# Moving SBUF addresses: the first x pair beside the weight chunks, kvs 32 bytes on, and weight chunks at a pitch of 4128 bytes instead of 4096

## The chip, the cores and the metric

The kernel runs on one core of a Trainium2 chip. The metric is the device time of one execution in microseconds; for the kernel before the median of three runs is 907.83 us (906.24 to 909.28). One more execution was taken with the hardware profiler, and the trace and the profile's page are of that one.

## The reference

An attention without a score matrix is followed by a two-layer feed-forward network. With batch 8, 8 heads, 576 positions and head size 64, and all in float32:

```
q_s = softmax(q, over d);  k_s = softmax(k, over positions)
kv  = einsum('bhsd,bhse->bhde', k_s, v)        # 64 x 64 for each head
x   = einsum('bhsd,bhde->bhse', q_s, kv)       # to [4608, 512]
out = max(x @ w_in, 0)**2 @ w_out              # 512 -> 2048 -> 512
```

## The kernel before

**Precision.** TensorE's fast four-byte type, float32r, keeps fewer bits than float32. So each operand of the network is split into a high part and a low remainder, and every product is made of three matmuls: high by high, low by high, high by low. A product costs three matmuls of 128x128 weights by 512 columns.

**Blocks.** The 4608 positions are handled in nine blocks of 512: block b (0 to 7) is the first 512 positions of batch b, and block 8 gathers the 64 positions left over of each batch. A block has 16 steps, one for each slice `fc` of 128 of the 2048 hidden features. A step has two halves of 12 matmuls. In the first, `ffn_h` with `h_part` (lines 406 to 408), the weights in the array are 128x128 slices of the chunk `wi[fc]`, and the moving operand is the block's x: `x_hi` in lines 406 and 408, `x_lo` in line 407, four slices `cc` each. In the second, `ffn_out` (lines 440 to 442), the weights in the array are slices of the activations `g_hi` and `g_lo`, and the moving operand is the chunk `wo[fc]`. So a chunk `wi` is what is loaded into the array, and a chunk `wo` is what streams through it. The two halves of a step belong to slices two apart (`LAG`).

**Two x pairs.** `x_hi` and `x_lo` exist twice. Blocks 0, 2, 4, 6 and 8 read the first pair, `x_hi0` and `x_lo0`, blocks 1, 3, 5 and 7 the second one, `x_hi1` and `x_lo1`. The attention of batch b runs in the steps of block b-1 and writes the other pair. Its matmuls are those of lines 299 (k by v, plain float32) and 378 (q by kv, with `kvs` as the weights and `qs` as the moving operand, 320 or 256 columns), put between the steps' matmuls by the table `slots`. Block 7's steps hold the gathering of the leftovers and no attention; block 8 holds neither.

**Weights.** Each of the 32 chunks (16 `wi`, 16 `wo`) is loaded once as raw float64 words, turned into a float32 and split into a high half (2048 bytes per partition) and a low half (2048 bytes) in the same place; this happens during the attention of batch 0 and in block 0. In order of loading the chunks are i0, i1, i2, i3, o2, i4, o3, i5, o0, i6, o1, i7, o4, i8, o5, i9, o6, i10, o7, i11, o8, i12, o9, i13, o10, i14, o11, i15, o12, o13, o14, o15; call that place n, from 0 to 31.

**Where the tiles lie.** A tile takes the same bytes in every partition. Pools lie one behind another in the order in which they are opened, and the tiles in a pool in the order of their first use, each rounded up to 32 bytes. From the sizes one can count, per partition:

- the 32 chunks lie end to end at a pitch of 4096 bytes;
- `x_hi0`, the first tile of the pool `const`, lies 79,008 bytes below the first chunk, which is 32 bytes off a multiple of 64; `x_lo0` follows after 8192 bytes;
- `x_hi1` and `x_lo1` lie right behind the last chunk, 131,072 and 139,264 bytes above the first chunk, both multiples of 4096;
- the tiles `g_hi`, `g_lo` and `qs` lie at multiples of 64 bytes from the first chunk; `kvs` lies 46,112 bytes below it, again 32 off a multiple of 64.

`qe`, the transposed q of pairs 1 and 3 of batch 0, is a tile of the pool `first` (2304 bytes), the topmost; `w_pool` has a tag `raw` of four buffers of 2560 bytes through which passing tiles go (`left`, `xf`, `tb`, `xs`, `o`).

Of the kernel before, what the change touches and what calls it, by code (L numbers as in the profile page):

```python
# [8 lines left out]
F32 = mybir.dt.float32  # L9
F32R = mybir.dt.float32r  # L10
U32 = mybir.dt.uint32
# [5 lines left out]
P = 128  # L17
# [7 lines left out]
RAWB, WB = 4, 3  # L25
EARLY_SPLITS = [("o",2),("o",3),("i",4),("o",0)]
OFFSET = 100
AHEAD = 4
EARLY = 8
PRE = 4  # L30
# [12 lines left out]
def attention_ffn_kernel(ctx: ExitStack, tc: tile.TileContext, q, k, v, w_in, w_out, out):  # L43
    nc = tc.nc

    B, H, S, D = q.shape
    DM, DF = w_in.shape
    NPAIR = H // 2
    NCC = DM // P
    NFC = DF // P  # L50
    NT = 512
# [3 lines left out]
    const = ctx.enter_context(tc.tile_pool(name="const", bufs=1))  # L55
    work = ctx.enter_context(tc.tile_pool(name="work", bufs=2))
    attn_pool = ctx.enter_context(tc.tile_pool(name="attn", bufs=2))
    w_pool = ctx.enter_context(tc.tile_pool(name="weights", bufs=2))
    dram = ctx.enter_context(tc.tile_pool(name="dram", bufs=1, space=bass.MemoryType.DRAM))
    ps_a = ctx.enter_context(tc.tile_pool(name="ps_a", bufs=1, space=bass.MemoryType.PSUM))  # L60


    stay = ctx.enter_context(tc.tile_pool(name="stay", bufs=1))
    raws, wi, wo = {}, {}, {}
    x_hi = [const.tile([P, NCC, NT], F32R, name="x_hi0")]
    x_lo = [const.tile([P, NCC, NT], F32R, name="x_lo0")]
    x_left = dram.tile([P, NCC, B * LEFT], F32, name="x_left")


# [10 lines left out]
    def next_bank(who):  # L80
        n = taken[who]
        taken[who] += 1
        return banks[{"first": n % 3, "h": n % 2, "a": 2 + n % 2}[who]]

    kvs = const.tile([P, 2, P], F32R, name="kvs")
    qT = const.tile([P, 4, LOW, BLK], F32, name="qT")
    ident = const.tile([P, P], F32, name="ident")
    start = ExitStack()
    first = start.enter_context(tc.tile_pool(name="first", bufs=1))
    ps_first = start.enter_context(tc.tile_pool(name="ps_first", bufs=2, space=bass.MemoryType.PSUM))  # L90
    for i in range(NB, NPAIR):
        kt.append(first.tile([P, 2, LOW, D], F32, name=f"kt{i}"))
        vt.append(first.tile([P, 2, LOW, D], F32, name=f"vt{i}"))
        qt.append(first.tile([P, 2, LOW, D], F32, name=f"qt{i}"))
    ones = const.tile([P, 1], F32, name="ones")

    v0 = [t.rearrange("p h j d -> p (h j d)")[:, : 2 * LOW * D].rearrange("p (h j d) -> p h j d", h=2, j=LOW) for t in vt]

# [38 lines left out]
    def load_pair(b, pr):  # L137
        for n in range(3):
            load_one(b, pr, n)

    chunks, last = [], []

    def load_w(part, fc):
        raw = stay.tile([P, 512, 2], U32, name=f"raw_{part}{fc}", tag=f"{part}{fc}")
        if part == "i":
            src = w_in[:, fc * P : (fc + 1) * P].bitcast(U32).rearrange("(cc p) f -> p cc f", p=P)
            nc.sync.dma_start(raw.rearrange("p (cc f) w -> p cc (f w)", cc=NCC), src)
        else:
            nc.sync.dma_start(raw.rearrange("p f w -> p (f w)"), w_out[fc * P : (fc + 1) * P, :].bitcast(U32))
        raws[part, fc] = raw  # L150

    def split_weight(part, fc):

        raw = raws[part, fc]
        low, high = raw[:, :, 0], raw[:, :, 1]
        w = w_pool.tile([P, 512], U32, name="w", bufs=WB)
        wf = w.bitcast(F32)

        with ExitStack() as order:
            if his:
                order.enter_context(tc.issue_after(his[-1].ins))
            nc.scalar.activation(low, raw.bitcast(U8)[:, :, 3], AF.Copy, scale=1 / 32, bias=-15.5 / 32)
        t = banks[3]
        nc.scalar.activation(t, high.bitcast(F32), AF.Copy, scale=2.0**-112)
        t = t.bitcast(U32)
        nc.vector.scalar_tensor_tensor(out=t, in0=t, scalar=3, in1=low, op0=ALU.logical_shift_left, op1=ALU.bitwise_or)
        nc.vector.scalar_tensor_tensor(out=w, in0=high, scalar=0x80000000, in1=t, op0=ALU.bitwise_and, op1=ALU.bitwise_or)  # L169
        finish_split()  # L170
        chunk = stay.tile([P, 2, 512], F32R, name=f"w{part}{fc}", tag=f"{part}{fc}")
        chunks.append(chunk)
        (wi if part == "i" else wo)[fc] = chunk

        def parts():
            his.append(nc.scalar.copy(chunk[:, 0], wf))
            nc.gpsimd.tensor_tensor(chunk[:, 1], wf, chunk[:, 0].bitcast(F32), op=ALU.subtract)  # L177

        unsplit.append(parts)
# [3 lines left out]
    def finish_split():  # L183
        while unsplit:
            unsplit.pop()()
# [5 lines left out]
    def ordered(f, *args):  # L191

        with ExitStack() as order:
            if last:
                order.enter_context(tc.issue_after(last[-1].ins))
            return f(*args)

    def attention(b, pr):

        n = b * NPAIR + pr  # L200
# [5 lines left out]
        st = {}  # L206
        odd = early and n % 2 == 1

        def bank(cols):
            if b == 0 and odd:  # L210
                t = ps_first.tile([P, NT], F32, name="first_ps", tag="a")
            else:
                t = next_bank("first" if b == 1 else "a") if b else banks[2]
            return t[:, :cols]
# [120 lines left out]
        def q_t_early(j0, j1):  # L335
            def go():
                qn = st["qn"]
                if "q" not in st:
                    if b == 0 and odd:
                        st["q"] = first.tile([P, S], F32, name="qe")  # L340
                    else:
                        st["q"] = qT.rearrange("p g j a -> p (g j a)")[:, :S]
                c0, c1 = j0 * P, min(j1 * P, S)
                ps = bank(c1 - c0)
                for j in range(j0, j1):
                    if j < HIGH:
                        mm = nc.tensor.transpose(ps[:, j * P : (j + 1) * P], qn[:, j], ident)
                    else:
                        mm = nc.tensor.transpose(ps, qn[:HALF, HIGH], ident[:HALF, :HALF])
                if b:  # L350
                    last.append(mm)
                nc.scalar.copy(st["q"][:, c0:c1], ps)
            return go
# [128 lines left out]
    for c in LOADS:  # L482
        i = int(c[1])
        if c[0] == "w":
            load_w("i", i)
        else:
            load_one(0, i, "kqv".index(c[0]))
    order0 = list(range(2, PRE)) + list(range(min(2, PRE))) + list(range(PRE, NFC))

    def load_more(n):  # L490
        load_w("o", order0[n])
        if n + PRE < NFC:
            load_w("i", order0[n + PRE])

    for n in range(AHEAD):
        load_more(n)
    for t in range(len(us[0]) + SKEW * (NPAIR - 1)):
        for pr in range(NPAIR):
            n = t - SKEW * pr
            if 0 <= n < len(us[pr]):  # L500
                with tc.high_priority(OFFSET):
                    us[pr][n]()
                if n == 4:
                    split_weight("i", pr)
                    if pr == NPAIR - 1:
                        for c in EARLY_SPLITS:
                            split_weight(*c)
                if n == 7:
                    finish_split()
                    for fc in range(min(PRE, pr + 1)):  # L510
                        for cc in [pr] if fc < pr else range(pr + 1):
                            h_part(hs[fc], 0, fc, cc)
# [6 lines left out]
    for pr in range(NB):  # L519
        load_pair(1, pr)  # L520
    for n in range(AHEAD, NFC):
        load_more(n)
# [24 lines left out]
    def in_slot(i):  # L547
        for u in slots.get(i, []):
            if i < 2 * NFC:
                with tc.high_priority(OFFSET):  # L550
                    ordered(u)
# [3 lines left out]
    for n in range(len(steps) + LAG):  # L555
        if n < len(steps):
            blk, fc = steps[n]
            if n < PRE:
                gs[n] = activate(hs[fc], blk, fc)
            else:  # L560
                gs[n] = ordered(ffn_h, blk, fc) if blk == 0 else ffn_h(blk, fc)
            if blk == 0:
                for x in [n + 4] if n else range(5):
                    if PRE <= x < NFC and order0[x] not in wi:
                        split_weight("i", order0[x])
                for x in [n + 2] if n else range(3):
                    if x < NFC and order0[x] not in wo:
                        split_weight("o", order0[x])
                finish_split()
        m = n - LAG  # L570
        in_slot(2 * n)
        if m >= 0:
            b2, f2 = steps[m]
            if m % NFC == 0:
                accs[b2] = [ps_o.tile([P, DM], F32, name=f"o_ps{t}", tag="o") for t in range(4)]
            args = b2, f2, gs.pop(m), accs[b2], m % NFC
            ordered(ffn_out, *args) if b2 == 0 else ffn_out(*args)
        in_slot(2 * n + 1)
# [30 lines left out]
```

## Time and profile before

| | |
|---|---|
| median of the runs | 907.83 us |
| profiled execution, first to last instruction | 903.5 us |
| PE busy | 876.7 us (97%) |
| DVE, ACT, POOL busy | 579.4, 408.2, 201.9 us |
| mean granted TensorE clock | 0.991 |

The profiled span is 4.3 us below the median of the runs, which also holds what lies around the instructions. PE is TensorE's matmul, PEld its weight load, DVE VectorE, ACT ScalarE, POOL GpSimd. A matmul's record reaches until its results have drained, so records of neighbours overlap; what counts for the time is the distance from one start to the next.

### The profile page before, as it was taken

What the parts mean: (1) busy time and instruction counts of PE and PEld (TensorE: products, weight loads), DVE (VectorE), ACT (ScalarE), POOL (GpSimd) and SP (SyncE); (2) the same over time, 40 slices, a digit from 0 to 9 for tenths busy, and PEclk for the clock granted to TensorE, in tenths of its full rate; (3) what the DMA queues carried; (4) which work ended last, traced back from release to release, by engine and by line L of the source; (5) the groups of instructions that cost most, each with busy time, mean ns of one, the idle gap of its engine ahead of it and who ended that gap; (6) DMA issues with size and microseconds to landing.
All of it is one profiled execution on the core that took longest, in us unless ns stands there. A gap on an engine that the chain in (4) does not pass through costs nothing.

```text
span 903.5 us, 12672 instructions
## 1 busy us (share of the span) xinstructions
PE 876.7 (97%) x4368; PEld 703.5 (78%) x4368; DVE 579.4 (64%) x1177; ACT 408.2 (45%) x801; POOL 201.9 (22%) x177
## 2 busy tenths in 40 slices
PE   4898999999999999999999999999999999999997
PEld 3576677888878888888888888888888888888885
DVE  6767797877778776877688768876764242222222
ACT  3876765455444444544454444444444232222222
POOL 3666535222213220231122212221222000000000
PEclk9989999999999999999999999999999999999999
DMA  9898212422142223322333133222311030001001
GB/s 244 269 320 248 59 37 56 118 72 83 44 117 73 79 60 101 87 70 71 88 84 81 49 80 91 85 57 68 93 31 32 3 93 1 1 1 46 1 1 46
DMA packets 95743, 73.18 MB, mean 81 GB/s; under 512 B 47552, under 2 KB 85440, under 8 KB 95680
## 3 DMA queue, kind: packets, MB, share of 16 engines
q1 hardware_dynamic: 94944, 71.53, 28.9%
q10 hardware_dynamic: 736, 0.85, 0.4%
q8 instruction: 34, 0.56, 0.3%
q14 instruction: 29, 0.24, 0.1%
HBM read 54.00 MB, written 18.35 MB: 80 GB/s over the span
## 4 chain that ended last, share of the span: by engine, by line
PE 91%; DVE 3%; DMA 2%; issue 2%; ACT 1%; POOL 0%; SPq 0%; DVEq 0%; POOLq 0%; ACTq 0%
PE o_ps L440 14%; PE bank L406 14%; PE o_ps L441 14%; PE o_ps L442 14%; PE bank L407 14%; PE bank L408 14%; PE bank L299 2%; PE bank L378 1%; DMA kt<-in_k_dram 1%; DMA vt<-in_v_dram 1%; DMA qt<-in_q_dram 1%; DVE w L169 1%; PE bank L358 0%; DVE m L218 0%; PE first_ps L299 0%
## 5 line engine op out<-in xcount | busy, mean ns | idle before, releaser
L406 PE MATMUL bank<-x_hi,wi 128*128 128x512 f32 x568 | 227.2, 401 | 2.8 <-ACT x_hi L188 2.2
L440 PE MATMUL o_ps<-wo,g_hi 128*128 128x512 f32 x576 | 228.1, 398 | 0.8 <-ACT g_hi L419 0.8
L441 PE MATMUL o_ps<-wo,g_hi 128*128 128x512 f32 x576 | 226.4, 393 | 0.0
L407 PE MATMUL bank<-x_lo,wi 128*128 128x512 f32 x568 | 225.6, 397 | 0.0
L408 PE MATMUL bank<-x_hi,wi 128*128 128x512 f32 x568 | 225.0, 396 | 0.0
L442 PE MATMUL o_ps<-wo,g_lo 128*128 128x512 f32 x576 | 224.8, 392 | 0.0
L418 DVE TENSOR_TENSOR r<-r 128x512 f32<-128x512 f32 x128 | 112.6, 880 | 122.4 <-ACT r L412 122.1
L423 DVE TENSOR_TENSOR g_lo<-r,g_hi 128x512 fp32r<-128x512 f32 x132 | 99.8, 756 | 105.3 <-ACT g_hi L419 103.9
L419 ACT CAST g_hi<-r 128x512 fp32r<-128x512 f32 x144 | 89.2, 619 | 127.8 <-PE o_ps L441 80.8
L412 ACT ACTIVATE r<-bank 128x512 f32<-128x512 f32 x142 | 84.8, 598 | 111.1 <-PE bank L408 103.7
L406 PEld LDWEIGHTS bank<-x_hi,wi 128*128 128x128 f32 x568 | 107.3, 189 | 29.2 <-ACT x_hi L188 3.6
L440 PEld LDWEIGHTS o_ps<-wo,g_hi 128*128 128x128 f32 x576 | 108.6, 189 | 25.9 <-ACT g_hi L419 1.0
L408 PEld LDWEIGHTS bank<-x_hi,wi 128*128 128x128 f32 x568 | 107.7, 190 | 24.8 <-POOL wi L177 0.5
L442 PEld LDWEIGHTS o_ps<-wo,g_lo 128*128 128x128 f32 x576 | 108.4, 188 | 23.1
L441 PEld LDWEIGHTS o_ps<-wo,g_hi 128*128 128x128 f32 x576 | 108.6, 188 | 23.0 <-issue 0.2
L407 PEld LDWEIGHTS bank<-x_lo,wi 128*128 128x128 f32 x568 | 107.6, 189 | 22.7 <-issue 0.2
L389 POOL TENSOR_TENSOR x_lo<-xf,x_hi 128x256 fp32r<-128x256 f32 x48 | 39.0, 813 | 378.1 <-ACT x_hi L388 377.4
L332 POOL TENSOR_TENSOR qs<-qT,qs 64x640 fp32r<-64x640 f32 x48 | 81.9, 1707 | 58.7 <-ACT qs L331 47.3
L218 DVE TENSOR_REDUCE m<-kt 128x128 f32<-128x640 f32 x32 | 41.4, 1298 | 18.9 <-DMA kt<-in_k_dram 18.9
L331 ACT CAST qs<-qT 64x640 fp32r<-64x640 f32 x48 | 34.8, 726 | 37.4 <-DMA qT<-bounce 36.0
L380 ACT COPY xf<-bank 64x320 f32<-64x320 f32 (+1 forms) x96 | 37.9, 395 | 22.1 <-PE bank L378 14.8
L265 ACT ACTIVATE qn<-qn 128x640 f32<-128x640 f32 x32 | 23.6, 739 | 50.1 <-DVE qn L262 42.9
(118 smaller groups left out, 773.5 us busy)
## 6 DMA issues: line engine op xcount, KB each, us to landing
out_dram<-o SPq DMA_DIRECT2D x70, 128.0 KB, 2.4
raw_i<-in_moe_w_in_dram SPq DMA_DIRECT2D x16, 512.0 KB, 9.5
raw_o<-in_moe_w_out_dram SPq DMA_DIRECT2D x16, 512.0 KB, 9.6
bounce<-tb SPq DMA_DIRECT2D x24, 320.0 KB, 2.2
qT<-bounce SPq DMA_DIRECT2D x96, 80.0 KB, 2.2
kt<-in_k_dram SPq DMA_DIRECT2D x32, 160.0 KB, 3.0
qt<-in_q_dram SPq DMA_DIRECT2D x30, 160.0 KB, 2.9
vt<-in_v_dram SPq DMA_DIRECT2D x56, 80.0 KB, 2.5
```

The lines of the kernel that those rows point to most:

```text
L218: nc.vector.tensor_reduce(m, kk.rearrange("p h j d -> p h d j"), axis=AX.X, op=ALU.max)
L332: nc.gpsimd.tensor_tensor(qs[other], qT[own], qs[own].bitcast(F32), op=ALU.subtract)
L406: nc.tensor.matmul(ps, wi[fc][:, 0, sl], xh[:, cc, :], start=(cc == 0), stop=False)
L407: nc.tensor.matmul(ps, wi[fc][:, 0, sl], xl[:, cc, :], start=False, stop=False)
L408: last.append(nc.tensor.matmul(ps, wi[fc][:, 1, sl], xh[:, cc, :], start=False, stop=(cc == NCC - 1)))
L412: nc.scalar.activation(r, ps, AF.Relu)
L418: nc.vector.tensor_tensor(r, r, r, op=ALU.mult)
L419: gh = nc.scalar.copy(g_hi, r)
L423: e.tensor_tensor(g_lo, r, g_hi.bitcast(F32), op=ALU.subtract)
L440: nc.tensor.matmul(acc[t], g_hi[:, ts], wo[fc][:, 0], start=(n == 0), stop=False)
L441: nc.tensor.matmul(acc[t], g_hi[:, ts], wo[fc][:, 1], start=False, stop=False)
L442: prev = nc.tensor.matmul(acc[t], g_lo[:, ts], wo[fc][:, 0], start=False, stop=(n == NFC - 1))
```

## The change

`x_hi0` and `x_lo0` move from `const` to a pool of their own, `moving`, opened just ahead of the chunks' pool `stay`. `ones` is made ahead of `kvs`, so `kvs` moves on by 32 bytes against its neighbours. Each chunk gets a slot of 4128 bytes, and in the sixteen slots from n = 16 on it begins 16 bytes into its slot. `qe` becomes a passing tile under the tag `raw`.

```diff
+STAGGER = 8
...
+    moving = ctx.enter_context(tc.tile_pool(name="moving", bufs=1))
     stay = ctx.enter_context(tc.tile_pool(name="stay", bufs=1))
...
-    x_hi = [const.tile([P, NCC, NT], F32R, name="x_hi0")]
-    x_lo = [const.tile([P, NCC, NT], F32R, name="x_lo0")]
+    x_hi, x_lo = [], []
...
+    x_hi.append(moving.tile([P, NCC, NT], F32R, name="x_hi0"))
+    x_lo.append(moving.tile([P, NCC, NT], F32R, name="x_lo0"))
+    ones = const.tile([P, 1], F32, name="ones")
     kvs = const.tile([P, 2, P], F32R, name="kvs")
...
-    ones = const.tile([P, 1], F32, name="ones")
...
+    def place(part, fc, name, dtype):
+        n = places.setdefault((part, fc), len(places))
+        t = stay.tile([P, 2 * 512 + STAGGER], dtype, name=name, tag=f"{part}{fc}")
+        at = STAGGER // 2 if n >= NFC else 0
+        return t[:, at : at + 2 * 512]
...
-        raw = stay.tile([P, 512, 2], U32, name=f"raw_{part}{fc}", tag=f"{part}{fc}")
+        raw = place(part, fc, f"raw_{part}{fc}", U32).rearrange("p (f w) -> p f w", w=2)
...
-        chunk = stay.tile([P, 2, 512], F32R, name=f"w{part}{fc}", tag=f"{part}{fc}")
+        chunk = place(part, fc, f"w{part}{fc}", F32R).rearrange("p (n f) -> p n f", n=2)
...
-                        st["q"] = first.tile([P, S], F32, name="qe")
+                        st["q"] = w_pool.tile([P, S], F32, name="qe", tag="raw", bufs=RAWB)
```

No instruction is added or taken away, and no loop changes. Counted as above, the distances become: `x_hi0` 16,384 and `x_lo0` 8192 bytes below the first chunk, `kvs` 62,464 bytes below it, `x_hi1` and `x_lo1` 132,096 and 140,288 bytes above it, all multiples of 64, as those of `g_hi`, `g_lo` and `qs` stay. Chunk n lies 4128 n bytes above the first, and 16 more from n = 16 on. So against x, g and kvs, modulo 64: the chunks of even n below 16 (i0, i2, o0 to o5) lie at 0, those of odd n below 16 (i1, i3 to i9) at 32, those of even n from 16 on (o6 to o12, o14) at 16, and those of odd n from 17 on (i10 to i15, o13, o15) at 48.

More of the change, by code (lines that the diff above doesn't have):

```diff
@@ L141, in attention_ffn_kernel @@
     chunks, last = [], []
+    places = {}
+    def place(part, fc, name, dtype):
[3 more added lines that the diff above has]
+        return t[:, at : at + 2 * 512]
     def load_w(part, fc):
-        raw = stay.tile([P, 512, 2], U32, name=f"raw_{part}{fc}", tag=f"{part}{fc}")
+        raw = place(part, fc, f"raw_{part}{fc}", U32).rearrange("p (f w) -> p f w", w=2)
         if part == "i":
```

## The prediction

> **What bounds the kernel now.** I read the page first: busy time (part 1), then the chain that ended last (part 4).
>
> ```profile
> span 903.5 us, 12672 instructions
> PE 876.7 (97%) x4368; PEld 703.5 (78%) x4368; DVE 579.4 (64%) x1177; ACT 408.2 (45%) x801; POOL 201.9 (22%) x177
> ...
> PE 91%; DVE 3%; DMA 2%; issue 2%; ACT 1%; POOL 0%; SPq 0%; DVEq 0%; POOLq 0%; ACTq 0%
> ```
>
> PE is busy for 97% of the span and makes 91% of the chain. No instruction is added or removed, so only a matmul's length can move the time. Next, the view by stretches, cut at the first L406 of each of blocks 2 to 8 (from:to, length, then busy us and instructions of PE, PEld, DVE, ACT, POOL, granted clock, DMA share, GB/s):
>
> ```profile
> 243.67:338.64 94.97, 94.97 (x482) 76.58 (x480) 71.95 (x155) 44.34 (x90) 19.78 (x17) 1.00 0.29 78
> 338.64:432.29 93.65, 93.65 (x482) 76.55 (x481) 71.20 (x155) 44.34 (x90) 19.49 (x17) 1.00 0.30 79
> 432.29:527.26 94.97, 94.97 (x482) 76.58 (x480) 72.39 (x155) 44.54 (x90) 20.39 (x17) 1.00 0.29 78
> 527.26:620.91 93.65, 93.65 (x482) 76.54 (x481) 72.12 (x155) 44.39 (x90) 20.20 (x17) 1.00 0.29 80
> 620.91:715.87 94.96, 94.96 (x481) 76.58 (x480) 52.46 (x101) 41.11 (x86) 17.18 (x15) 1.00 0.17 43
> 715.87:802.91 87.04, 87.04 (x385) 72.07 (x384) 25.96 (x38) 22.91 (x39) 0.00 (x0) 1.00 0.10 25
> ```
>
> PE never idles here, at full clock. Blocks 2, 4 and 6, which read the first x pair, take 94.97, 94.97 and 94.96 us; blocks 3 and 5, with the same attention between their steps but the second pair, take 93.65. The same instructions are 1.32 us dearer on the first pair. Block 7, bare of attention, takes 87.04 us for 384 matmuls: 226.7 ns each.
>
> The view by lines shows it for one matmul (count, busy us, mean ns of one record), first in block 7, then in block 8:
>
> ```profile
> L406 PE MATMUL bank<-x_hi,wi 128*128 128x512 f32 x48 | 18.7, 389 | 0.0
> L407 PE MATMUL bank<-x_lo,wi 128*128 128x512 f32 x48 | 18.7, 389 | 0.0
> L441 PE MATMUL o_ps<-wo,g_hi 128*128 128x512 f32 x47 | 18.3, 389 | 0.0
> ```
> ```profile
> L408 PE MATMUL bank<-x_hi,wi 128*128 128x512 f32 x63 | 25.0, 397 | 0.0
> L407 PE MATMUL bank<-x_lo,wi 128*128 128x512 f32 x63 | 25.0, 397 | 0.0
> L406 PE MATMUL bank<-x_hi,wi 128*128 128x512 f32 x63 | 24.9, 396 | 0.0
> L441 PE MATMUL o_ps<-wo,g_hi 128*128 128x512 f32 x61 | 24.0, 394 | 0.0
> ```
>
> Shapes and chunks are the same; only the place of x differs. With x 32 bytes off a multiple of 64 from the chunks, an h matmul's record is 8 ns longer (397 against 389), and the out matmuls behind it are up to 5 ns longer though they never read x. The timeline (start, us, engine, line) gives the starts of the halves of one clean step and of one slow step:
>
> ```profile
> 792.03 0.39 PE L406 MATMUL bank<-x_hi,wi 128*128 128x512 f32 x1
> ...
> 794.75 0.39 PE L440 MATMUL o_ps<-wo,g_hi 128*128 128x512 f32 x1
> ...
> 797.47 0.39 PE L406 MATMUL bank<-x_hi,wi 128*128 128x512 f32 x1
> ...
> 802.91 0.40 PE L406 MATMUL bank<-x_hi,wi 128*128 128x512 f32 x1
> ...
> 805.73 0.40 PE L440 MATMUL o_ps<-wo,g_hi 128*128 128x512 f32 x1
> ...
> 808.48 0.40 PE L406 MATMUL bank<-x_hi,wi 128*128 128x512 f32 x1
> ```
>
> Clean: 2.72 + 2.72 = 5.44 us. Slow: 2.82 + 2.75 = 5.57 us.
>
> One more stretch tells what the 226.7 ns hold: block 0 right after a wait, where the clock is down.
>
> ```profile
> 85.39 0.63 PE L407 MATMUL bank<-x_lo,wi 128*128 128x512 f32 x1
> ...
> 87.95 0.63 PE L407 MATMUL bank<-x_lo,wi 128*128 128x512 f32 x1
> ```
>
> and, by the view by stretches,
>
> ```profile
> 85.40:87.90 2.50, 2.50 (x7) 1.98 (x6) 2.50 (x4) 0.00 (x0) 0.00 (x0) 0.50 0.45 103
> ```
>
> Six matmuls lie between these two starts, and at a granted clock of 0.50 the first pair's matmuls so start (87.95 - 85.39) / 6 = 0.427 us apart, with a weight load under each as ever. At full clock the same columns would take half, 213.3 ns. So of the clean 226.7 ns some 13.3 ns, and of the slow 235 ns some 21 ns, appear only at full clock: the array waits for its operands, by an amount that depends on addresses.
>
> The Trainium skill speaks against that. Its page "TensorE: Matmul & The Clock Gate", section "Step-by-step: what each phase is for", says that weights are loaded through a read port of their own and take nothing from the running matmul. By that rule no address matters here and the time stays. The 389 and 397 ns of the two blocks do not agree with it.
>
> **The change, part by part** (differences against the profiled span; the median lies 4.3 us above it, and I add them to the median).
>
> *First x pair.* At a multiple of 64 from the first chunk it stands as the second pair does. If its matmuls take the second pair's cadence, blocks 2, 4 and 6 give 3 x 1.32 = 3.96 us. Block 8 has 16 steps of 5.57 instead of 5.44: 2.1 us. In block 0 PE also waits for others, so I take 1.0, below the 1.32 of its like. Sum: -7.1 us.
>
> *kvs.* Block 3's 93.65 us are 6.61 more than block 7's. The q-by-kv matmuls have 8 x 320 + 8 x 256 columns, nine full matmuls of 213.3 ns, and 16 times 13.3 ns: 2.13 us. The k-by-v groups are four, and the timeline prices one:
>
> ```profile
> 405.94 0.39 PE L408 MATMUL bank<-x_hi,wi 128*128 128x512 f32 x1
> ...
> 406.26 0.80 PE L299 MATMUL bank<-vt,ke 128*64 128x65 f32 x20
> ...
> 406.99 0.50 PE L440 MATMUL o_ps<-wo,g_hi 128*128 128x512 f32 x1
> ...
> 407.32 0.39 PE L441 MATMUL o_ps<-wo,g_hi 128*128 128x512 f32 x1
> ```
>
> From 405.94 to 407.32 are 1.38 us, less two clean matmuls 0.93, by four 3.71. What is left, 6.61 - 2.13 - 3.71 = 0.77 us a block, is the cadence being off behind each interruption. In six blocks that is 4.6 us; some of it comes from kvs standing 32 off, some from the interruption itself. Between 0 and 4.6 I take half: -2.3 us.
>
> *Odd chunks below n = 16.* The eight chunks i1 and i3 to i9 now stand 32 off x, in all nine blocks: 8 x 12 x 9 = 864 h matmuls. The two nearest rows are the first pair's 8 ns (also 32 off, but there the moving tile was displaced) and the second pair's 0 (the moving tile stays where it was). I take the middle, 4 ns: +3.5 us, and 0.8 for the out matmuls behind them, half of (2.75 - 2.72) / 12 = 2.5 ns over 6 x 12 x 9 = 648. Ends: 0 and +8.5.
>
> *Chunks 16 bytes off.* i10 to i15 are loaded under x (6 x 12 x 9 = 648 matmuls), and o6 to o15 stream under g (10 x 12 x 9 = 1080): 1728. No row has a pair apart by an odd multiple of 16. The ends are -13.3 ns (nothing but the 512 columns is left) and +8 ns (the first pair's price): -23.0 to +13.8 us. Neither row is nearer, so I take the middle, -2.65 ns: -4.6 us.
>
> On the floor there is a figure from elsewhere: the Trainium skill, same page, section "Wait — 56ns, not 53.3ns?", gives 215.7 ns from start to start for 512 columns warm; by it the low end would be -11 instead of -13.3 ns and the middle -1.5 ns, -2.6 us, and the sum 900.
>
> *Loads, splits, qe.* The chunks' DMAs write the same bytes 16 or 32 further. If the upper sixteen, 16 x 512 KB = 8.4 MB, took a tenth longer, that would be 3.4 us at the 246 GB/s of the first row here, and it would lie ahead of a stretch with room:
>
> ```profile
> 50.00:100.00 50.00, 46.36 (x245) 35.65 (x244) 35.61 (x64) 34.16 (x66) 31.47 (x28) 0.96 0.82 246
> 100.00:150.00 50.00, 47.16 (x223) 35.89 (x222) 42.73 (x91) 34.53 (x65) 25.70 (x19) 0.97 0.19 52
> ```
>
> From 100 us on the DMA share is 0.19; without that room the 3.4 us would stand in block 0. I cost it at 0. `qe` has four buffers to pass through instead of one of its own; in batch 0 only the four small `left` tiles use them too, so its copy waits for nothing new, and pair 3's no longer for pair 1's. At nothing; without that cover, one copy and a transpose, under 1 us.
>
> Sum: -7.1 - 2.3 + 4.3 - 4.6 = -9.7 us: 898.
>
> **The rivals.**
>
> *The shift spoils the clean cadence (slower).* 226.7 ns is a cadence into which a run of like pairs settles; behind a disturbance it is missing, as the out halves of block 8 show. With 24 of 32 chunks displaced, the halves of a step no longer match each other. If every displaced pair costs the first pair's 8 ns: +8.5 + 13.8 - 7.1 - 2.3 = +12.9 us, 921; milder, 912 to 921. It decides from +4.5 ns a matmul for the 1728 on (-9.4 + 4.3 + 7.8 = +2.7 us). For it: the first pair is a displaced pair and is dear. Against it: x, g and kvs keep one place.
>
> *16 bytes off is free of the wait (much faster).* Then -7.1 - 2.3 + 4.3 - 23.0 = -28 us, 880; with the odd chunks at no cost too, 875. For it: the half-clock rows show that the wait is not in the array. Against it: no row at full clock has it.
>
> *It does nothing.* The difference of the two pairs comes from something other than their place modulo 64 (their distance from the chunks, say), or gain and loss cancel: 905 to 911, about 908. This is also where the page's rule ends; against it stand the 1.32 us, three times over.
>
> **How the numbers follow.** The forecast, 898 with its own range of 889 to 905, gets 0.38. Free 16 bytes: 0.25. Nothing: 0.13. Slower: 0.24. About 0.3%, 2.7 us, is what a measurement of this kernel can tell from no change; so faster is 0.38 + 0.25 = 0.63, same 0.13, slower 0.24. The range reaches from 879 (the free case, 880, and a little beyond) to 916 (the slower case with the odd chunks at 8 ns and the 1728 at 5: -9.4 + 8.5 + 8.6 = +7.7).
>
> **What would show it.** In the changed kernel's view by stretches, blocks 2, 4 and 6 should come to what blocks 3 and 5 take, and the sixteen steps of block 8 should fall below 5.57 us each; by lines, L406 to L408 should read 389 in block 8 for i0 and i2, near 393 for i3 to i9. The records of the steps with o6 to o15 and i10 to i15 decide the rest: below 389 for the faster rivals, 395 and more for the slower one. Blocks 3, 5 and 7 above 93.65 and 87.04 would mean that the shift spoils what was clean. I am wrong if block 8 does not shorten, if PE starts to wait in block 0, or if the shifted chunks' matmuls leave the bounds of -13.3 and +8 ns.

## The result, and the profile after

The changed kernel takes 920.48 us (median of 4 runs, 919.84 to 921.02); the kernel before, run beside it, 907.04 (905.95 to 909.28). The ratio is 1.0143, with a 95% interval of 1.0126 to 1.016: slower. The forecast was 898, the range 879 to 916.

The page of the kernel after: its first line, the first row of busy times and the shares of the chain.

```profile
span 917.9 us, 12671 instructions
...
PE 886.3 (97%) x4368; PEld 705.3 (77%) x4368; DVE 579.3 (63%) x1177; ACT 408.8 (45%) x801; POOL 202.9 (22%) x177
...
PE 85%; DMA 6%; DVE 5%; SPq 2%; issue 1%; ACT 1%; DVEq 0%; ACTq 0%
```

The span is 14.4 us longer. PE is busy 9.6 us longer with the same 4368 matmuls, and DMA and DVE have 11% of the chain instead of 5%. PE's idle time grows too, from 26.8 to 31.6 us. So there are two losses: dearer matmuls, and a start in which PE waits for others. The view by stretches, cut at the first L417 (L406 before) of blocks 2, 3, 6 and 7, columns as in the prediction:

```profile
252.54:347.59 95.05, 95.05 (x482) 76.64 (x480) 71.25 (x154) 44.60 (x90) 19.54 (x16) 1.00 0.30 78
347.59:442.64 95.05, 95.05 (x482) 76.66 (x481) 70.31 (x155) 44.33 (x90) 18.70 (x16) 1.00 0.30 78
...
632.73:727.78 95.05, 95.05 (x481) 76.66 (x480) 51.82 (x100) 41.06 (x86) 17.05 (x14) 1.00 0.17 43
727.78:817.04 89.26, 89.26 (x385) 72.18 (x384) 25.99 (x38) 22.84 (x39) 0.00 (x0) 1.00 0.10 24
```

Every attention block now takes 95.05 us. Blocks 2, 4 and 6 (94.97 before) gained nothing, blocks 3 and 5 (93.65 before) lost 1.40 each, and block 7, the cleanest, went from 87.04 to 89.26: 232.4 ns a matmul instead of 226.7, at full clock and with PE never idle. Block 8, by the timeline from its first L417 to the one fourteen steps later:

```profile
817.04 0.40 PE L417 MATMUL bank<-x_hi,wi 128*128 128x512 f32 x1
...
895.12 0.39 PE L417 MATMUL bank<-x_hi,wi 128*128 128x512 f32 x1
```

78.08 / 14 = 5.58 us a step: no better than the 5.57 before. The view by lines for block 7 says the same of single matmuls:

```profile
L453 PE MATMUL o_ps<-wo,g_lo 128*128 128x512 f32 x65 | 25.7, 395 | 0.0
L452 PE MATMUL o_ps<-wo,g_hi 128*128 128x512 f32 x64 | 25.3, 395 | 0.0
L418 PE MATMUL bank<-x_lo,wi 128*128 128x512 f32 x64 | 25.3, 395 | 0.0
```

389 ns before, 395 now, in both halves of a step alike. (Records overlap and their ends are modelled, so these lengths only echo the 226.7 and 232.4 ns from start to start.)

The rest of the loss lies ahead. Block 1 begins at 154.76 us instead of 147.26 (+7.5), block 2 at 252.54 instead of 243.67 (+8.9, the last 1.4 being block 1's own matmuls). From block 2 to the end it is 917.9 - 252.54 = 665.4 instead of 659.8 us (+5.5).

### The profile page after: what moved, and what is told of

Read it like the earlier page. It is cut to its first block, busy times and chain, and to the rows that moved or that the text cites. A ratio compares the mean times of both kernels' runs of the same rounds, so it can differ in the third digit from the quotient of the medians.

```text
span 917.9 us, 12671 instructions
## 1 busy us (share of the span) xinstructions
PE 886.3 (97%) x4368; PEld 705.3 (77%) x4368; DVE 579.3 (63%) x1177; ACT 408.8 (45%) x801; POOL 202.9 (22%) x177
## 4 chain that ended last, share of the span: by engine, by line
PE 85%; DMA 6%; DVE 5%; SPq 2%; issue 1%; ACT 1%; DVEq 0%; ACTq 0%
PE o_ps L451 14%; PE bank L417 14%; PE o_ps L452 14%; PE o_ps L453 14%; PE bank L419 13%; PE bank L418 13%; DMA kt<-in_k_dram 2%; PE bank L310 2%; DMA qt<-in_q_dram 2%; PE bank L389 1%; DMA raw_o<-in_moe_w_out_dram 1%; DMA raw_i<-in_moe_w_in_dram 1%; DVE w L180 1%; DVE m L229 1%; DVE m L248 1%
## 5 line engine op out<-in xcount | busy, mean ns | idle before, releaser
L417 PE MATMUL bank<-x_hi,wi 128*128 128x512 f32 x568 | 228.1, 403 | 5.4 <-DVE kvn L326 2.4
L429 DVE TENSOR_TENSOR r<-r 128x512 f32<-128x512 f32 x128 | 107.8, 842 | 126.3 <-ACT r L423 126.0
L417 PEld LDWEIGHTS bank<-x_hi,wi 128*128 128x128 f32 x568 | 107.4, 189 | 31.9 <-DVE kvn L326 2.6
```

Source lines behind the costliest of these rows:

```text
L417: nc.tensor.matmul(ps, wi[fc][:, 0, sl], xh[:, cc, :], start=(cc == 0), stop=False)
L429: nc.vector.tensor_tensor(r, r, r, op=ALU.mult)
```

## The experiments

All start from the kernel before or after and change one thing. The table splits each profiled execution at the start of block 1, where PE no longer waits for loads, splits or attention of batch 0; the columns are microseconds, the last one with the kernel before beside it, and (1) for a single run. "Old" and "new" say in which order the scheduler, the program that lays out the instructions, hands the early ones to the engines: e1, e2, e8 to e10 and e12 to e14 have exactly the order of before on PE, DVE, ACT and POOL, e3 to e6 exactly that of after. The start of block 1 is that of one execution, and it varies from one to the next: the span of the kernel before lay between 900.0 and 907.7 us in its executions. The columns behind it repeat far better (659.8 us in before and e3, 660.2 in e15 and e16, whose operands stand alike), so small differences are read from them.

| kernel | early order | block 1 starts | block 2 to end | block 7 | median, before |
|---|---|---|---|---|---|
| before | old | 147.3 | 659.8 | 87.04 | |
| after | new | 154.8 | 665.4 | 89.26 | 920.48, 907.04 |
| e1_x_only | old | 145.6 | 654.0 | 87.04 | 897.93 (1), 905.93 |
| e2_x_kvs | old | 148.3 | 654.0 | 87.04 | 900.46, 904.43 |
| e3_qe_only | new | 157.8 | 659.8 | 87.04 | 915.07, 904.43 |
| e4_no_stagger | new | 152.5 | 653.2 | 87.04 | 907.08, 904.43 |
| e5_pitch_only | new | 153.9 | 665.5 | 89.22 | 919.10, 904.43 |
| e6_mod64 | new | 154.5 | 662.8 | 88.72 | 916.74 (1), 906.25 |
| e8_all16 | old | 145.3 | 663.9 | 88.39 | 908.45 (1), 906.25 |
| e9_all32 | old | 146.6 | 665.2 | 89.12 | 911.60 (1), 906.25 |
| e10_abs0 | old | 147.0 | 653.6 | 87.04 | 899.02 (1), 906.25 |
| e12_all256 | old | 148.5 | 653.6 | 87.04 | 900.36 (1), 905.93 |
| e13_all128 | old | 146.6 | 665.3 | 89.13 | 911.63 (1), 905.93 |
| e14_qs256 | old | 145.6 | 652.5 | 87.04 | 897.99, 905.93 |
| e15_qe_left_apart | a third | 152.8 | 660.2 | 87.04 | 910.88, 906.72 |
| e16_left_only | a fourth | 177.5 | 660.2 | 87.04 | 932.87, 906.72 |

### The parts of the change by themselves: e2, e3, e4, e5

**e2_x_kvs**: the kernel before with the first x pair and `kvs` moved as in the change; chunks at a pitch of 4096, `qe` in `first`.

```diff
+    moving = ctx.enter_context(tc.tile_pool(name="moving", bufs=1))
...
-    x_hi = [const.tile([P, NCC, NT], F32R, name="x_hi0")]
...
+    x_hi.append(moving.tile([P, NCC, NT], F32R, name="x_hi0"))
...
+    ones = const.tile([P, 1], F32, name="ones")
     kvs = const.tile([P, 2, P], F32R, name="kvs")
...
```

> Only the first x pair and kvs move, with the chunks at a pitch of 4096 bytes and qe in a tile of its own; all operands then stand at like places modulo 64. Theory A (the clean 226.7 ns start to start needs a whole run of like pairs): blocks 2, 4 and 6 take 93.7 us or less, block 8 takes 87.0 in place of 89, block 1 begins where it did (147 us), and the time falls by 7 to 12 us, to 895 to 900. Rival B (the first pair is slow for its distance from the chunks or for another reason than its place modulo 64): 907, blocks 2, 4 and 6 at 95.0 us.

Measured: 0.994 (0.9919 to 0.996), faster. By stretches, blocks 2, 5 and 7:

```profile
244.61:338.68 94.07, 93.89 (x482) 76.38 (x481) 72.16 (x155) 44.35 (x90) 21.72 (x17) 1.00 0.30 79
526.09:619.61 93.52, 93.52 (x482) 76.53 (x480) 73.58 (x156) 44.46 (x91) 21.89 (x17) 1.00 0.30 80
713.12:800.16 87.04, 87.04 (x386) 72.07 (x385) 25.97 (x38) 22.90 (x39) 0.00 (x0) 1.00 0.10 25
```

The whole tail from block 2 on is 5.8 us shorter than before, and blocks 4 to 6 take 0.13 us less than blocks 3 and 5 did. So the direction is as expected, but the size is not: the medians fall by 4.0 us, where 7 to 12 were expected and the prediction had costed the two moves at 9.4. Blocks 2 and 3 (94.07 and 93.89) stay above the 93.52 of their like; why was not followed up.

**e3_qe_only**: the kernel before with `qe` in the passing tiles.

```diff
-                        st["q"] = first.tile([P, S], F32, name="qe")
+                        st["q"] = w_pool.tile([P, S], F32, name="qe", tag="raw", bufs=RAWB)
```

> The kernel before with qe as a passing tile and nothing else; no matmul operand of blocks 1 to 8 moves. Theory A2 (block 0's delay of 7.5 us comes from the order of the first instructions, which the scheduler lays out anew when qe has another tile): the first L406 of block 1 starts at 153 to 156 us in place of 147.3, and the time is 913 to 916; blocks 2 to 8 as before. Rival B2 (the delay comes from writing the chunks to shifted places, or from the slower matmuls of block 0): block 1 starts at 147 us, time 907.

Measured: 1.0109 (1.0082 to 1.0135). No operand of the network has moved, and the tail is before's, 659.8 us. All of the loss lies ahead of block 1, 10.5 us in the trace, where 6 to 9 were expected; the time, 915.07 us, is in the expected range. The stretch by whose end the first part of it has arisen, before:

```profile
50.00:60.00 10.00, 8.82 (x37) 6.82 (x36) 6.74 (x12) 7.17 (x14) 6.31 (x7) 0.95 1.03 366
```

and in e3:

```profile
50.00:60.00 10.00, 8.31 (x28) 5.74 (x27) 2.95 (x6) 2.91 (x6) 3.03 (x4) 0.82 1.01 356
```

DVE, ACT and POOL do less than half of their work here, and PE 28 matmuls instead of 37, at a lower granted clock; the DMA engines are as busy as before. e3's view of waits for 46 to 60 us (engine, line, releaser: us, times, longest):

```profile
POOL g_lo L423 <- ACT g_hi L419: 6.9, 1, 6.9
DVE x_lo L189 <- ACT x_hi L188: 4.3, 1, 4.3
ACT x_hi L188 <- PE first_ps L358: 4.1, 1, 4.1
```

In the kernel before the first of these is 3.0 us and the others are not among the waits of this stretch:

```profile
POOL g_lo L423 <- ACT g_hi L419: 3.0, 1, 3.0
```

e3's timeline shows what stands in front:

```profile
52.02 0.63 PE L408 MATMUL h_ps<-x_hi,wi 128*128 128x512 f32 x1
52.45 1.79 PE L358 MATMUL first_ps<-qe,kvn 128*128 128x512 f32 x4
...
59.59 0.47 PE L440 MATMUL o_ps<-wo,g_hi 128*128 128x512 f32 x1 [0.80 <-ACT g_hi L419]
```

L358, the product of `qe` with its kv, now stands on PE behind eight L407 and L408 at 0.43 us each; ACT waits 4.1 us for it with its `x_hi`, and the weights' next splits (L164) start on ACT only behind that, at 60.00 us instead of 55.41. The first out matmul of this stretch, before:

```profile
54.99 0.47 PE L440 MATMUL o_ps<-wo,g_hi 128*128 128x512 f32 x1 [0.80 <-ACT g_hi L419]
```

is 4.6 us earlier. That is less than half of the loss: the 250th matmul on PE starts 4.6 us later than before (56.0 against 51.4), the 700th 10.5 us later (158.0 against 147.5). The other 6 us come in between, and were not followed to one wait. A stretch of it in e3, with PE idle at times and at a lower granted clock (before: 60 matmuls, clock 1.00):

```profile
90.00:100.00 10.00, 7.93 (x26) 6.37 (x27) 5.54 (x13) 5.71 (x11) 5.34 (x5) 0.66 0.03 7
```

The tag brings another order of the early instructions, and the first part of the loss is seen in it.

**e4_no_stagger**: the kernel after with the chunks end to end, so the x pair, `kvs` and `qe` as in the change.

```diff
-STAGGER = 8
+STAGGER = 0
```

> The changed kernel with STAGGER = 0: x, kvs and qe as changed, chunks at a pitch of 4096 bytes. Theory A with A2: block 1 starts at 153 to 156 us, all later blocks at the clean cadence (block 7 at 87.0 us, block 8 the same), time 902 to 907. Rival C (the slower cadence of the changed kernel comes from the moved x pair or kvs, not from the chunks): block 7 at 89.3 us as in the changed kernel, time 918 to 921.

Measured: 1.0021 (1.0005 to 1.0038), 907.08 us, and block 1 at 152.5 us, each just outside what was expected. Block 7:

```profile
716.34:803.38 87.04, 87.04 (x386) 72.07 (x384) 26.00 (x38) 22.90 (x39) 0.00 (x0) 1.00 0.10 25
```

Against e2, which has the old order, 6.6 us are lost, and the tail is 0.8 us shorter: the start alone loses. Against the kernel after, the tail is 12.2 us shorter (653.2 and 665.4): that is the price, from block 2 on, of the longer slots with the 16 bytes. (The medians, 907.08 and 920.48, were not taken side by side: the kernel before took 904.43 beside one and 907.04 beside the other.)

**e5_pitch_only**: the kernel after without the 16 bytes; the slots stay at 4128.

```diff
-        at = STAGGER // 2 if n >= NFC else 0
+        at = 0
```

> The changed kernel without the 16 bytes: all chunks begin at the start of their slots of 4128 bytes, so odd chunks stand 32 off modulo 64 and even ones at 0. Theory A: the halves of a step are still unlike, so block 7 stays near 89 us (mean start to start 230 to 233 ns in both halves), time 916 to 921. Rival D (the 16 bytes are what costs; 32 off costs little): block 7 at 87.5 us or less, time 906 to 912.

Measured: 1.0158 (1.0131 to 1.0185), 919.1 us. Tail and block 7 (665.5 and 89.22 us) are the kernel after's. Against e4, beside the same runs of the kernel before, it loses 12.0 us. The 16 bytes, on which the prediction spent its widest term, change the tail by 0.1 us; the 32 bytes of pitch do the rest.

**e1_x_only**: the x pair alone; the edit is e2's without the `ones` line.

> The kernel before with the first x pair alone moved to just below the chunks; kvs stays 32 bytes off. The prediction's step for x: 7.1 us less than before, so about 899 to 901 us, and blocks 2 to 6 still some 0.9 us longer when they hold attention matmuls than in e2 (2.3 to 4.6 us in all) if kvs counts; if kvs does not count, the same blocks as e2 to 0.2 us.

Measured: 897.93 us in one run, 1 us below the expected range. A block with attention in e1, then in e2 (above, 526.09):

```profile
523.19:616.84 93.65, 93.65 (x482) 76.55 (x480) 72.90 (x156) 44.30 (x90) 21.21 (x17) 1.00 0.30 80
```

93.65 against 93.52: `kvs` gives 0.13 us a block, 0.8 in six, where 0.9 a block was the figure if it counts. The tails are equal all the same (654.0), since e2's blocks 2 and 3 are longer, and the 2.5 us between the two totals is block 1's start (145.6 and 148.3).

### Which distance is the clean one: e6, e10, e12, e13, and e8, e9

The theory of the prediction: an operand is clean at a multiple of 64 from the other. Rivals: the period is longer, or it is likeness from one matmul to the next that counts, or the absolute place.

**e6_mod64**: the kernel after with the odd chunks 32 bytes into their slots and no 16, so that every chunk is a multiple of 64 from x and g.

```diff
-        at = STAGGER // 2 if n >= NFC else 0
+        at = STAGGER if n % 2 else 0
```

> The changed kernel, slots of 4128 bytes, but odd chunks begin 32 bytes into their slots and no chunk has the 16: every chunk is again at a multiple of 64 from x, g and kvs, while the distances modulo 128 and above differ from chunk to chunk. Theory A (place modulo 64 is what counts): block 7 takes 87.0 us, mean start to start 226.7 ns in both halves, time 903 to 908 (with the delay that qe's tile gives block 0). Rival E (the unequal pitch as such costs, since banks repeat at a larger distance than 64): block 7 between 88 and 89.5 us, time 912 to 920.

Measured: 916.74 us; block 7:

```profile
725.85:814.57 88.72, 88.72 (x386) 72.08 (x384) 25.96 (x38) 22.84 (x39) 0.00 (x0) 1.00 0.10 24
```

The theory falls: at multiples of 64 throughout, a matmul still takes 88.72 / 384 = 231.0 ns. The rival's times came out; the banks that it gives as its reason are shown by no run.

**e10_abs0**: e2 with 32 empty bytes at the foot of `const`; all operands move together.

```diff
+    const.tile([P, 8], F32, name="spacer")
```

> The kernel e2_x_kvs with one spacer of 32 bytes at the foot of the pool: every operand moves by 32, so all stand at absolute addresses that are multiples of 64, still alike among each other. Theory A (only the difference of the two operands counts): blocks 7 and 8 at 87.0 us, time 898 to 902. Rival G (the absolute place counts: tiles at an odd multiple of 32 are the good ones, as the slow pair before stood at a multiple of 64): blocks 7 and 8 at 89 us or more, time 912 to 920.

Measured: 899.02 us, block 7 at 87.04 as in e2. Moving everything together by 32 bytes changes nothing. In e5 the `wi` chunks i1, i6, i10 and i14 stand 32 bytes further too, but x does not, and there they take 232.5 to 233.4 ns a matmul in blocks 7 and 8. So it is the distance that counts, as far as these places tell.

**e8_all16** and **e9_all32**: e2 with the x and g tiles 16 and 32 bytes further in, by cutting them from longer tiles.

```diff
+    def inset(pool, n, name, by):
+        return pool.tile([P, n + 16], F32R, name=name)[:, by : by + n]
...
```

> The kernel e2_x_kvs with both x pairs and the g tiles 16 bytes further: every matmul of lines 406 to 442 now pairs a moving tile and a loaded tile 16 off modulo 64, all alike. Theory A in its narrow form (a run of like pairs settles, whatever the offset): block 7 settles at a steady start to start, 87.0 us or another constant. Theory A in its wide form (the offset has to be 0): no settling, 88.5 to 90 us as in the changed kernel. Rival F (16 bytes off is free of the wait): 82.0 to 85 us, time 870 to 890.

> The kernel e2_x_kvs with both x pairs and the g tiles 32 bytes further: every matmul of lines 406 to 442 pairs tiles 32 off modulo 64, in both halves of a step. Narrow form of theory A (likeness is enough): block 7 settles at one start to start, near 87.0 us. Wide form (the offset itself costs, as it did for the first x pair before): 89.5 to 90.3 us for blocks 7 and 8, 234 ns a matmul, time 918 to 925.

Measured: 908.45 and 911.6 us, block 7 at 88.39 and 89.12. They don't answer the question of likeness: each longer tile pushed the next one 64 bytes on, so the distances were not the same from tile to tile. They show only that these two mixtures are not clean, with one exception that comes up below.

**e12_all256** and **e13_all128** ask it again with gaps between the pools: 256 (128) empty bytes ahead of the chunks, 256 (384) ahead of the second x pair.

```diff
+    moving.tile([P, 64], F32, name="gap0")
...
+    late.tile([P, 64], F32, name="gap1")
```

> The kernel of e2 with 256 empty bytes between the first x pair and the chunks and 256 more below the second x pair: every distance between the operands of the FFN matmuls is 256 modulo 512 instead of 0; the order of the instructions stays e2's. Theory P (the clean cadence needs a distance that is a multiple of 256 bytes): blocks 7 and 8 stay at 226.7 to 227 ns a matmul, 87.0 to 87.2 us for each, span 898 to 900 us. Rival (only operands that start at the same place modulo 512 or 4096 run clean): 228.5 ns or more, 87.7 us or more a block, span 903 us or more.

> The same with 128 empty bytes below the chunks and 384 below the second x pair: every distance is 128 modulo 256, the same one at all matmuls of the FFN. It repeats with a sound layout what e8 and e9 were meant to ask. Theory P: near 233 ns a matmul in both halves, 89.0 to 89.6 us for blocks 7 and 8, span about 912 to 916 us. Rival L (it is the change of the distance from matmul to matmul that costs; one that is the same at all of them runs clean, whatever it is): 226.7 ns, 87.0 us, span about 899 us.

Measured: 900.36 and 911.63 us; only e13's span, 909.7 us, lies 2 us below what was expected. Block 7 of e12:

```profile
712.87:799.91 87.04, 87.04 (x386) 72.07 (x384) 25.97 (x38) 22.87 (x39) 0.00 (x0) 1.00 0.10 25
```

and of e13:

```profile
719.56:808.69 89.13, 89.13 (x385) 72.25 (x384) 25.94 (x38) 22.88 (x39) 0.00 (x0) 1.00 0.10 24
```

One kernel, one order, one distance throughout; only 256 or 128 differs, and a matmul takes 226.7 or 89.13 / 384 = 232.1 ns. The same 389 and 395 ns by lines, e12's first out matmuls and e13's:

```profile
L443 PE MATMUL o_ps<-wo,g_hi 128*128 128x512 f32 x64 | 24.9, 389 | 0.0
```

```profile
L443 PE MATMUL o_ps<-wo,g_hi 128*128 128x512 f32 x64 | 25.3, 395 | 0.0
```

Likeness alone is not enough: of the distances held throughout, 0 and 256 bytes modulo 512 run clean, 128 modulo 256 does not. A multiple of 64 does not do, then; a multiple of 256 bytes does. By that, `x_hi0` stood 79,008 = 308 x 256 + 160 bytes away in the kernel before, 160 off. In the kernel after chunk n stands 32 n bytes off, and 16 more from n = 16 on: only n = 0 and 8 (i0 and o0) stand at a multiple of 256. In e5 four chunks do (n = 0, 8, 16 and 24), in e6 eight, and e6 has the shorter tail (662.8 against 665.5 us).

The traces of the mixed kernels price single chunks, since the twelve matmuls of a half all use one. In e6's block 7, the starts of three halves with i9 (a multiple of 256), o7 and i10 (64 off):

```profile
775.78 0.39 PE L417 MATMUL bank<-x_hi,wi 128*128 128x512 f32 x1
...
778.50 0.40 PE L451 MATMUL o_ps<-wo,g_hi 128*128 128x512 f32 x1
...
781.27 0.39 PE L417 MATMUL bank<-x_hi,wi 128*128 128x512 f32 x1
...
784.06 0.39 PE L451 MATMUL o_ps<-wo,g_hi 128*128 128x512 f32 x1
```

The halves take 2.72, 2.77 and 2.79 us: the clean time stands right beside dear ones. In e6's blocks 7 and 8 exactly the eight chunks at a multiple of 256 (i0, i5, i9, i13, o0, o6, o10 and o15) come back to 226 or 227 ns by the end of their half, and no other does.

But a multiple of 256 is not enough by itself in a mixture: over after, e5 and e6, blocks 7 and 8, halves at a multiple of 256 take 226.6 to 231.6 ns a matmul, all others 228.8 to 236.2, and i0 in the kernel after takes 229.9. What ran just before counts as well. The kernel before shows it in block 8, where the h halves are dear and the out halves stand at a multiple of 256. The first and the ninth matmul of an out half, and the start of the next half:

```profile
805.73 0.40 PE L440 MATMUL o_ps<-wo,g_hi 128*128 128x512 f32 x1
...
807.58 0.39 PE L442 MATMUL o_ps<-wo,g_lo 128*128 128x512 f32 x1
...
808.48 0.40 PE L406 MATMUL bank<-x_hi,wi 128*128 128x512 f32 x1
```

The first eight take 1.85 us, 231 ns each, the last four 0.90 us, the clean pace again. So behind a dear half the clean cadence comes back after some eight matmuls. That would explain why, in a mixture, chunks that stand right are dear too.

One row stands against a strict rule. In e8 the out half of o6 has its operands 16 and 144 bytes off a multiple of 256. Its first matmul and the next half's, in block 7 and then in block 8:

```profile
764.17 0.40 PE L445 MATMUL o_ps<-wo,g_hi 128*128 128x512 f32 x1
...
766.90 0.39 PE L411 MATMUL bank<-x_hi,wi 128*128 128x512 f32 x1
...
853.00 0.40 PE L445 MATMUL o_ps<-wo,g_hi 128*128 128x512 f32 x1
...
855.80 0.39 PE L411 MATMUL bank<-x_hi,wi 128*128 128x512 f32 x1
```

In block 7 it takes 2.73 us, nearly the clean time, and so do most out halves of even number there; in block 8, behind another x pair, 2.80 us with the same operands. So the clean pace can occur off a multiple of 256 too. What the runs show is that it holds when all distances are multiples of 256; that it needs them is not shown.

### One step further: e14

The moving operands of the attention's q-by-kv matmuls (`qs0` and `qs1`, called `qs` in the views) still lie 128 off a multiple of 256. **e14_qs256** is e2 with two small tiles, which bear the name `qs` as well and lie below them, taken from the pool behind, so that the two operands lie 128 bytes lower; nothing after them moves.

```diff
-            qs = attn_pool.tile([P, LOW * 2, 1], F32, name="qs")
+            qs = w_pool.tile([P, LOW * 2, 1], F32, name="qs", bufs=2)
```

> The kernel of e2 with the two small qs tiles taken from the pool behind, so that the moving operands of the attention's matmuls (q, 128 bytes beside a multiple of 256 from the chunks so far) start a multiple of 256 bytes from the chunks too; nothing else moves, and the order of the instructions stays e2's. Theory P: the stretches after each attention matmul in blocks 2 to 6 go, where 4.9 us lie over 226.7 ns a matmul in e2's trace: 1 to 3 us of them go, 897 to 900 us, 0.990 to 0.993 of the kernel before. Rival (these stretches come from the shape of the attention matmuls, not from where q lies): as e2, 0.994.

Measured: 0.9928 (0.99 to 0.9956), 897.99 us: the lowest ratio of all that were measured with an interval. A block with attention:

```profile
522.41:615.74 93.33, 93.33 (x481) 76.48 (x480) 72.69 (x156) 44.43 (x91) 22.81 (x18) 1.00 0.30 80
```

93.33 against e2's 93.52: 0.19 us in a block, 1.1 in six, the lower end of what was expected; most of the 4.9 us that lay over 226.7 ns a matmul stay. The totals could not tell e14 from e2, since the intervals of the two ratios overlap; block 1's start (145.6 and 148.3 us) differs by more than the blocks do. This version beats both kernels.

### Buffers or order: e15, e16

Sharing four buffers could itself have cost the time. **e15_qe_left_apart** is e3 with the `left` tiles in two buffers of their own; **e16_left_only** is the kernel before with `left` in one buffer of its own, `qe` untouched.

```diff
-                    left = w_pool.tile([P, LEFT], F32, name="left", tag="raw", bufs=RAWB)
+                    left = w_pool.tile([P, LEFT], F32, name="left", tag="left", bufs=2)
```

> The kernel before with qe in the passing tiles as in e3, and the small left tiles (which shared these four buffers with qe) in two buffers of their own. All operands of the FFN keep their distances modulo 256, so blocks 2 to 8 should stay as before to 0.3 us each. Theory B (qe makes others wait for one of the four shared buffers): block 1 starts at 146 to 149 us, time within 0.3% of the kernel before. Theory O (the new tag changes the order in which the scheduler hands the early instructions to the engines; no buffer is waited for): the order differs from before's and from e3's, and block 1 starts at another time than in both, anywhere from 143 to 160 us.

> The kernel before with the left tiles in a buffer of their own and qe where it was; the distances of the FFN stay the same modulo 256. Theory B: nothing, within 0.3% of before. Theory O: the early order changes again (this time without qe), and the start of block 1 moves by more than 1.5 us from 147.3 us, in either direction, with the time following it one for one.

Measured: 1.0051 (1.0031 to 1.0072) and 1.0283 (1.0264 to 1.0302); the tails are before's to 0.4 us. e15 starts block 1 at 152.8 us although `qe` shares with no `left` tile any more, and neither in e3 nor in e15 does anything wait for a store of `left`. So the theory of shared buffers falls for e3. e15 also tells where its loss comes from: `qe` is a passing tile as in e3, but PE has the order of before for its first 640 matmuls, and while it lasts next to nothing is lost. The 600th matmul starts at 126.4 us (126.2 before); the 700th, behind the change of order, at 151.4 (147.5 before). So the order is what is left as the cause; no run has e3's order with `qe` in a tile of its own. e16 was badly chosen: with one buffer it made a wait of its own, which hides what its order is worth. Its waits from 20 to 170 us:

```profile
ACT left L366 <- DMA x_left<-left: 19.6, 2, 14.9
PEld o_ps L440 <- ACT left L366: 17.1, 1, 17.1
```

It shows, at least, what a wait for these buffers looks like where there is one.

## Why the prediction was wrong

**The wrong sign came from two steps,** the price of the displaced chunks and the nothing for `qe`. The sum was -7.1 - 2.3 + 4.3 - 4.6 + 0. Measured:

- *First x pair, -7.1.* Right as far as it can be read. e1's tail is 5.8 us shorter than before's, where the prediction had 3.96 + 2.1 = 6.1 for blocks 2 to 8; its 1.0 for block 0 can't be told from the start's own spread. The reason given was wrong, though ("a multiple of 64 from the first chunk"): 16,384 and 8192 are multiples of 256, and 64 is not enough (e6, e13).
- *kvs, -2.3.* The middle of 0 to 4.6 was too large: -0.8 (e1 against e2, 0.13 us a block). Of the rest, another 1.1 belonged to `qs`, which the change leaves where it was.
- *Odd chunks and 16 bytes, +4.3 - 4.6.* This is the step that failed: "32 bytes off a multiple of 64 from the chunks" was taken for what makes the first pair dear, and worked through as 864 matmuls at 4 ns and 1728 at -2.65. Against this -0.3 stand +12.0 us by the medians (e5 against e4) and 12.2 by the tails (after 665.4 against 653.2). The rows behind it showed two places, a dear one and a clean one; the prediction took 64 for the period, and 160 off modulo 256 against 0 fits the same rows. With 64, half of the chunks below n = 16 stayed clean and the 16 bytes were something new that might be free. With 256 all but two are off, and the 16 bytes change nothing (e5). The price was mis-sized too: block 7's matmuls went up by 5.7 ns on average, and even the chunks at multiples of 64 (i0, i2, o0 to o5), which the sum charged with little or nothing, by 2.1 to 6.5 ns. The first bound, -13.3 ns, had no row but one at half clock; no run here went below 226.7 ns at full clock. The Trainium skill, page "TensorE: Matmul & The Clock Gate", section "Wait — 56ns, not 53.3ns?", gives 215.7 ns for it; none of these kernels, with a weight load under each matmul, reached that.
- *Loads and splits, nothing.* Right as far as the start's spread lets one see: block 1 begins at 152.5 us in e4 and at 153.9 in e5, which differ in the place of the chunks alone.
- *qe, nothing.* Also failed: "its copy waits for nothing new" is true, and e3 bears it out, but the tag changes the order of the early instructions, on PE alone at more than a hundred places. With that order 10.6 us are lost in e3 against before and 6.6 in e4 against e2. That the order does it is argued from e3's waits and from e15, not isolated. The nine kernels with the old order start block 1 between 145.3 and 148.5 us, the five with the new one between 152.5 and 157.8.

Together: -4.0 (e2 against before) + 6.6 (e4 against e2) + 12.0 (e5 against e4) = +14.7 us with the rounding, which is e5 against the same 904.43 us. The kernel after, in its own comparison beside 907.04, lost 13.4.

**The rivals.** "The shift spoils the clean cadence" is what happened, and 920.48 lies in its 912 to 921. Its mechanism held: the stretches that were clean (3, 5 and 7) lost most. Its price didn't: 22.3 us for the displaced chunks where 12.0 were lost, nothing for `qe` where 6.6 were, and -9.4 for x and `kvs` where -4.0 came. That these errors nearly cancel is luck. Its words about a cadence into which like pairs settle fit the traces: behind a dear half some eight matmuls pass before it is back. Against it stood "x, g and kvs keep one place", which counts for nothing, since it is the distance to the chunk that matters (e10, e13). "16 bytes off is free" fell with e5. The Trainium skill's rule that weights come through a read port of their own (the page and section named in the prediction), by which, as the prediction read it, no address would matter, does not agree with these runs either: e12 and e13 differ in nothing but a gap, and in 2.09 us in block 7.

**What the text said would show it** did: blocks 3, 5 and 7 rose above 93.65 and 87.04, block 8 did not shorten, and PE waited more (31.6 us idle instead of 26.8).

**Left open.** Why 256 bytes, of which part of the memory or the array, and why e8's even out halves run nearly clean in block 7, no run tells; held throughout, only 0 and 128 modulo 256 were run (and 160, for the first x pair of the kernel before), and the other distances are priced in mixtures alone. Nor is it known why the same new order loses 10.6 us in e3 and 6.6 in e4. Whether some order with `qe` in the passing tiles is as good as the old one was not tried.

## What to carry to other kernels

Where TensorE sets the time and each matmul has its own weight load, it is worth trying to put every moving operand a multiple of 256 bytes per partition from the weights loaded beside it, and to keep the pitch of weight tiles a multiple of 256: 32 bytes of padding cost 12 us of 907 here, 1.3%. Do it for all of them, since one dear operand slows the matmuls behind it too. When two places in a trace differ in price, list all the periods that fit them before giving a new place a price; a run with a gap tells them apart. A tile that changes its pool or tag can change the order of the instructions of a whole stage, so compare the orders, and not only who waits for the buffer.

## What the runs showed that was not expected

- The pace of a stream of 512-column float32r matmuls, each with a weight load, depends on the operands' distance: 226.7 ns at a multiple of 256 bytes (e2, e10, e12), 232.1 ns at 128 off throughout (e13), 231.0 at mixed multiples of 64 (e6), 232.4 at mixed multiples of 16 (after). Behind a dear half the clean cadence takes some eight matmuls to come back (before, block 8). One cadence was never beaten: block 7 takes 87.04 us to the hundredth in ten of the sixteen kernels.
- The start is sensitive out of proportion: with the same instructions, block 1 begins between 145.3 and 148.5 us in the nine kernels with the old order, between 152.5 and 157.8 in the five with the new one, and at 177.5 where a `left` buffer is short.
